# Keys and queries loaded as f32 by SyncE and cast by GpSimd, in place of GpSimd's casting loads

## The chip, the cores and the metric

The kernel runs on one core of one Trainium2 chip. A core has five engines with queues of their own: TensorE (PE in the profile; its weight loads are PEld) multiplies matrices, VectorE (DVE) and ScalarE (ACT) work on elements, GpSimd (POOL) does so too and can issue transfers, and SyncE (SP) issues transfers only. Every queue runs strictly in order, and engines wait for one another by semaphores. Transfers are carried by 16 DMA engines. The metric is the device time of one execution in microseconds (us): 232.63 us, the median of three runs (232.62 to 235.34).

## The reference

Two stages, in f32. Attention has a batch of 4, 8 heads, 768 positions and 64 values a head; heads 0, 2 and 6 see all earlier positions, the other five see the first 4 positions (the sinks) and a window of 64. A feed-forward block with a gate follows.

```python
scores = scale * np.matmul(q, k.transpose(0, 1, 3, 2))
causal = rel >= 0
stream_keep = causal & (is_sink | in_win)
scores = np.where(mask[None], scores, -1e9)
a = np.exp(scores - max); a = a / sum
attn = np.matmul(a, v)                       # (4, 8, 768, 64)
x = attn.transpose(0, 2, 1, 3).reshape(3072, 512)
h = x @ w_in                                 # 512 -> 2048
g = h * (1.0 / (1.0 + np.exp(-beta * h)))
return g @ w_out                             # 2048 -> 512, (3072, 512) f32
```

## The kernel before

**Units and chunks.** A chunk is one half (384 positions) of one batch; there are eight, 0 to 7. A chunk has four units, each a pair of heads p and p+4, so there are 32 units. For each unit the kernel needs keys and queries with the 64 head values on the partitions (transposed), in bf16. Scores are matmuls of transposed keys against transposed queries (L464 for units up to 11, L932 in groups for units 12 and up), exponents are taken on ScalarE (L472, L936), masks are multiplied in on VectorE (L437), the product with V (L495) is normed on VectorE (L498, L500) into x. x is transposed into xT, and the feed-forward block follows per chunk: first product (L560), tanh on ScalarE (L563), gate on VectorE (L566), second product (L604), output tile osb (L611 or L609), store (L614).

**How keys and queries arrive.** In chunks 0 to 2 they are loaded as f32 (`load_qk`, L138), cast to bf16 into `qkb` (`cast`, L296 on VectorE, L298 on GpSimd or ScalarE), and transposed by TensorE (L373). In chunks 3 to 7 they are loaded by GpSimd with a transfer that casts to bf16 on the way (`load_rows`, L330): 12 loads for a chunk, one for each of keys and queries, row block t of three, and half of the heads. They land in the rows tiles `ROWS[c % 2, name]`, two of which alternate. SyncE then issues transposing transfers from these rows into the key tile KT and the query tile QTD (`transposes_dma`, L341), six for a chunk, one for each of keys and queries and each t. A transposing transfer from SyncE also brings x to xT for units 8 and up, apart from unit 11 and the two units that end the program (`x_by_dma`, L511).

**What else stands on GpSimd.** V arrives as f32 by SyncE (`load_v`, L152, three loads of 256 KB for a chunk) and is cast into VX by GpSimd (L304; by VectorE for units 8 to 15). For the heads with a window, the sinks' keys are copied into KO (`sinks_of`, L356, L357, after the transposes), and the sinks' values into VO (L317, L318).

**What sets the order.** The order on every engine is written out by the program itself. A planned clock (`clock[0]`, in ns) goes forward by each TensorE step's planned cost. Work on other queues is put on a heap with a planned time (`later`, `event`) and is emitted once the clock has passed it. `rows_at` plans the loads of rows, `transposes_at` the transposes (never ahead of the rows' loads), `v_at` V's loads, `sinks_values` the sinks' copies and V's casts. From unit 12 on the scores are made in 13 groups, and what accompanies each is in a table of strings (SEQ). The planned times only set the order: on the chip each instruction runs when its queue reaches it and its semaphores allow it. TensorE's order is fixed in the same way. In the compiled program SyncE's transfers use eight completion semaphores in turn.

Chunk 3's scores are groups 0 to 2, chunk 4's 3 and 4, chunk 5's 5 and 6, chunk 6's 7 to 9, chunk 7's 10 to 12.

Of the kernel before, what the change touches and what calls it, by code (L numbers as in the profile page):

```python
# [17 lines left out]
def kernel(  # L18
# [13 lines left out]
    nc = tc.nc  # L32
# [253 lines left out]
    def cast(u, names=("k", "q"), on=None):  # L286
# [5 lines left out]
        for name in names:  # L292
            copy = on or nc.gpsimd.tensor_copy
            dst, src = s["qkb"][:, "qk".index(name)], staged[name, c, p // 2][:, p % 2]
            if copy == nc.vector.tensor_copy:
                copy(out=dst.rearrange("p t h d -> p h t d"), in_=src)  # L296
            else:
                copy(out=dst, in_=src.rearrange("p h t d -> p t h d"))  # L298
# [24 lines left out]

    def load_rows(c):

        b, h2 = chunks[c]

        def one(name, src, t, hh):
            r, w = h2 * HALF + t * 128, pos(b, hh) * D
            nc.gpsimd.dma_start(out=ROWS[c % 2, name][:, t].rearrange("p (a w) -> p a w", a=NPAIR)[:, :, w:w + D],  # L330
                                in_=src[b, hh * NPAIR:(hh + 1) * NPAIR, r:r + 128, :].rearrange("h p d -> p h d"))
        return [lambda n=n, src=src, t=t, hh=hh: one(n, src, t, hh) for n, src in (("k", k), ("q", q)) for t in range(HT) for hh in range(2)]
# [473 lines left out]
    rows3 = load_rows(3)  # L806
# [8 lines left out]
    for i in range(6):  # L815
        rows3[i]()
    for i in range(6, 9):
        later(1000 * (i - 3), rows3[i])
# [16 lines left out]
    def rows_at(at, some, gap=1000):  # L835
        for i, f in enumerate(some):
            event("rows", at + gap * i, f)

    def transposes_at(at, c, names=("k", "q"), gap=1300):
        for i, f in enumerate(transposes_dma(c, names)):  # L840
            f = event("transposes", at + gap * i, f, ("rows",))
# [3 lines left out]
    def v_at(at, c, tiles):  # L845
        for i in tiles:
            event("v", at + 2500 * i, lambda i=i: load_v(c, tiles=[i]))
# [6 lines left out]
    rows4 = load_rows(4)  # L854

    for t in range(8, 12):
# [4 lines left out]
        if t == 8:  # L861
            rows_at(1000, rows3[9:])
        if t == 9:
            transposes_at(0, 3, ("k",), 0)
        if t == 10:
            transposes_at(0, 3, ("q",), 0)
        if t == 10:
            rows_at(2000, rows4[0:4])
        if t == 11:
            rows_at(1000, rows4[4:8])  # L870
            for u in range(12, 16):
                sinks_values(u, 1000, 2000)
# [197 lines left out]
```

## Time and profile before

| | |
|---|---|
| median of three runs (lowest, highest) | 232.63 us (232.62, 235.34) |
| the profiled execution | 233.23 us |
| its span, from first to last instruction | 231.5 us |
| TensorE busy, granted clock | 218.4 us (94%), 1.0 |
| GpSimd busy, of it issues of the casting loads | 102.6 us, 45.0 us |
| read from and written to HBM | 27.27 MB, 6.29 MB |

One execution on the chip was recorded by the hardware profiler. The page gives each engine's busy time, then the span in 40 slices, then the chain of work that ended last, followed back from the last instruction, then the costliest groups of instructions. In a group's line stand the source line, the engine, the operation, what is written and read and in what shape (partitions x elements), how many, then the sum of their durations in us and the mean in ns, then the idle time of the engine just before them and what ended it. A line of the transfers gives KB each and the median us from issue to landing. In the timeline a line starts with the time of the start and the duration, both in us; SPq and POOLq are the queues of SyncE and GpSimd. In the tables by stretch, after the stretch and its length, come the busy times of TensorE, its weight loads, VectorE, ScalarE and GpSimd with the count of instructions, then the granted clock, the DMA share and GB/s. Matmuls are pipelined and their ends are modelled.

### The profile page before, as it was taken

The numbers are of one execution on the slowest core, as the hardware profiler recorded it, in microseconds if no ns is written. First come the engines' busy times: TensorE is split into PE (matmuls) and PEld (weight loads), VectorE is DVE, ScalarE is ACT, GpSimd is POOL, SyncE is SP. The second block draws the span as 40 slices with busy tenths as digits, with TensorE's granted clock in tenths as the row PEclk, the third lists the DMA queues.
The fourth block names the chain that finished last, engine by engine and source line by source line (L and its number), as shares of the span: only waits on it lengthen the run. The fifth ranks groups of instructions, "written<-read, shape, count | busy, mean of one in ns | idle before, by whom it ended". The sixth has DMA issues, their size and how long they took to land.

```text
span 231.5 us, 5309 instructions
## 1 busy us (share of the span) xinstructions
PE 218.4 (94%) x1939; PEld 131.5 (57%) x1960; DVE 143.7 (62%) x360; ACT 155.0 (67%) x303; POOL 102.6 (44%) x226
## 2 busy tenths in 40 slices
PE   7786799999999999999999999999999999999994
PEld 2675666555665566545654555454755555556553
DVE  6767578884968279835955594454781676338700
ACT  2897688866765798567875747775948797128621
POOL 6487760189619997219708793740042000000000
PEclk9999999999999999999999999999999999999999
DMA  6999999999999899994997999972732101211012
GB/s 193 258 302 192 165 168 219 222 225 227 193 148 137 115 139 144 125 218 109 152 191 126 146 184 140 143 136 71 172 64 62 50 0 45 77 50 50 0 45 91
DMA packets 96314, 31.78 MB, mean 137 GB/s; under 512 B 82704, under 2 KB 93344, under 8 KB 96288
## 3 DMA queue, kind: packets, MB, share of 16 engines
q0 software_dynamic: 35968, 8.13, 48.6%
q1 hardware_dynamic: 59456, 22.72, 47.9%
q10 hardware_dynamic: 864, 0.60, 0.8%
q8 instruction: 15, 0.25, 0.5%
q14 instruction: 11, 0.09, 0.2%
HBM read 27.27 MB, written 6.29 MB: 145 GB/s over the span
## 4 chain that ended last, share of the span: by engine, by line
PE 82%; DMA 4%; DVE 4%; issue 3%; ACT 3%; POOL 3%; POOLq 0%; ACTq 0%
PE mm L560 35%; PE tp L604 32%; PE po L495 5%; PE sp L932 5%; DMA w_in_sb<-in_moe_w_in_dram 4%; PE sp L464 2%; PE tp L587 2%; PE tp L373 1%; ACT es L936 1%; DVE es L437 1%; DVE x L500 1%; ACT es L472 1%; ACT th L563 1%; DVE KT L374 0%; PE tp L527 0%
## 5 line engine op out<-in xcount | busy, mean ns | idle before, releaser
L560 PE MATMUL mm<-xT,w_in_sb 128*128 128x384 bf16 x512 | 91.8, 326 | 1.8 <-DMA w_in_sb<-in_moe_w_in_dram 1.8
L563 ACT ACTIVATE th<-mm,beta_h 128x384 f32<-128x384 f32 x128 | 73.1, 598 | 22.1 <-PE mm L560 16.7
L604 PE MATMUL tp<-w_out_sb,gT 128*128 128x512 bf16 x347 | 86.5, 379 | 1.4 <-issue 0.3
L566 DVE SCALAR_TENSOR_TENSOR gT<-th,mm 128x384 bf16<-128x384 f32 x128 | 67.6, 551 | 30.5 <-ACT th L563 25.9
L560 PEld LDWEIGHTS <-w_in_sb 128*128 128x128 bf16 x512 | 48.0, 98 | 33.6 <-issue 2.2
L604 PEld LDWEIGHTS <-gT 128*128 128x128 bf16 x368 | 33.9, 98 | 33.6 <-issue 0.3
L936 ACT ACTIVATE es<-sp 128x512 bf16<-128x512 f32 (+1 forms) x84 | 39.9, 595 | 4.5 <-PE sp L932 4.5
L611 ACT ACTIVATE osb<-tp 128x512 f32<-128x512 f32 x21 | 12.7, 603 | 33.8 <-PE tp L604 30.5
L304 POOL CAST VX<-vs 128x384 bf16<-128x384 f32 x22 | 11.0, 508 | 36.7 <-DMA vs<-in_v_dram 32.2
L472 ACT ACTIVATE es<-sp 128x512 bf16<-128x512 f32 (+1 forms) x44 | 22.5, 561 | 4.3 <-PE sp L464 3.2
L495 PEld LDWEIGHTS <-es 128*128 128x128 bf16 x472 | 20.7, 97 | 7.8 <-issue 0.9
L330 POOL DMA_DIRECT2D s<-in_q_dram x30 | 22.5, 771 | 0.8 <-issue 0.6
L495 PE MATMUL po<-VX,es 128*128 128x65 bf16 x392 | 22.4, 193 | 0.3 <-DVE x L500 0.3
L330 POOL DMA_DIRECT2D s<-in_k_dram x30 | 22.5, 775 | 0.1
L437 DVE TENSOR_TENSOR es<-es,Mh 128x512 bf16<-128x512 bf16 (+3 forms) x58 | 19.5, 373 | 4.1 <-ACT es L936 3.7
L500 DVE TENSOR_TENSOR x<-po,rec 128x384 bf16<-128x384 f32 x32 | 17.8, 557 | 1.1
L464 PE MATMUL sp<-QTP,KT 128*128 128x128 bf16 (+2 forms) x113 | 16.6, 230 | 1.7 <-ACT es L472 0.9
L437 DVE TENSOR_TENSOR es<-es,Mc 128x384 bf16<-128x384 bf16 (+2 forms) x21 | 7.8, 374 | 11.4 <-ACT es L936 10.8
L498 DVE RECIPROCAL rec<-po 128x6 f32<-128x6 f32 x32 | 6.1, 192 | 13.2 <-PE po L495 13.1
L356 POOL COPY KO<-KT 128x128 bf16<-128x128 bf16 (+1 forms) x22 | 9.1, 412 | 9.6 <-DVE KT L374 5.5
L317 POOL COPY VO<-VX 128x128 bf16<-128x128 bf16 (+3 forms) x24 | 9.0, 374 | 8.6 <-DVE VX L304 7.6
L464 PEld LDWEIGHTS <-KT 128*128 128x128 bf16 x113 | 10.3, 98 | 3.6 <-issue 1.0
(75 smaller groups left out, 169.9 us busy)
## 6 DMA issues: line engine op xcount, KB each, us to landing
vs<-in_v_dram SPq DMA_DIRECT2D x24, 256.0 KB, 6.9
out_dram<-osb SPq DMA_DIRECT2D x23, 256.0 KB, 2.2
s<-in_k_dram SPq DMA_DIRECT2D x12, 192.0 KB, 4.3
w_in_sb<-in_moe_w_in_dram POOLq DMA_DIRECT2D x8, 256.0 KB, 8.3
w_out_sb<-in_moe_w_out_dram POOLq DMA_DIRECT2D x4, 512.0 KB, 11.1
s<-in_q_dram SPq DMA_DIRECT2D x10, 192.0 KB, 5.7
s<-in_k_dram POOLq DMA_DIRECT2D x30, 64.0 KB, 4.7
s<-in_q_dram POOLq DMA_DIRECT2D x30, 64.0 KB, 5.5
```

The source lines that it names most:

```text
L330: nc.gpsimd.dma_start(out=ROWS[c % 2, name][:, t].rearrange("p (a w) -> p a w", a=NPAIR)[:, :, w:w + D], in_=src[b, hh * NPAIR:(hh + 1) * ...
L437: nc.vector.tensor_mul(e, e, m)
L464: nc.tensor.matmul(sp[:, (i - lo) * 128:(j - lo) * 128], lhs, s["QT"][hh][:, q0 * 128:(q0 + j - i) * 128], start=True, stop=not added)
L472: nc.scalar.activation(out=es[:, 0:w], in_=sp[:, 0:w], func=ACTF.Exp, scale=scale)
L495: nc.tensor.matmul(po[:, qi, hh, :], e, val, start=(j == 0), stop=(j == len(lst) - 1))
L500: nc.vector.tensor_mul(x, po[:, :, :, 0:D], rec.to_broadcast([128, HT, 2, D]))
L560: nc.tensor.matmul(hp[:, 0:HALF], w_in_sb[:, mo, fi * 128:(fi + 1) * 128], xT[c][:, mo, :], start=(mo == 0), stop=(mo == MO - 1))
L563: nc.scalar.activation(out=th, in_=hp[:, 0:HALF], func=ACTF.Tanh, scale=beta_h[:, fi:fi + 1])
L566: nc.vector.scalar_tensor_tensor(out=gTs[c][:, fi, :], in0=th, scalar=1.0, in1=hp[:, 0:HALF], op0=ALU.add, op1=ALU.mult)
L604: nc.tensor.matmul(op, gTs[c][:, fi, ns * 128:(ns + 1) * 128], w_out_sb[:, fi, :], start=(fi == 0), stop=(fi == FO - 1))
L611: nc.scalar.activation(out=osb, in_=op, func=ACTF.Copy, scale=0.5)
L936: nc.scalar.activation(out=es[:, 0:w], in_=sp[:, 0:w], func=ACTF.Exp, scale=scale)
```

## The change

In chunks 3 to 7, `load_rows` no longer issues 12 casting loads on GpSimd. SyncE issues six f32 loads (keys and queries, three row blocks, all eight heads, 256 KB each), and GpSimd casts each to bf16 into the same rows tiles: one copy of 512 elements a partition, or, for the last batch (chunks 5 and 7), where the two halves of the heads change place, two copies of 256. Chunk 3's loads go into three small buffers (`fr`), which its keys and then its queries use; chunks 4 to 7 share one f32 tile each for keys and queries (`FROW`).

The planned times are written anew: chunk 3's keys are loaded ahead of its V, transposes wait for the casts instead of the loads, loads and casts of a chunk have times of their own (`chunk_at`), and the sinks' copies of a chunk come ahead of the next chunk's casts. V of chunk 4 is loaded at 75 instead of 88 us of planned time, with steps of 1.5 instead of 2.5 us. Last, `cast` uses one order of the axes on all engines: VectorE also writes its destination in one run and reads its source in the other order.

```diff
     def cast(u, names=("k", "q"), on=None):
...
-            if copy == nc.vector.tensor_copy:
-                copy(out=dst.rearrange("p t h d -> p h t d"), in_=src)
-            else:
-                copy(out=dst, in_=src.rearrange("p h t d -> p t h d"))
+            copy(out=s["qkb"][:, "qk".index(name)], in_=staged[name, c, p // 2][:, p % 2].rearrange("p h t d -> p t h d"))
...
     def load_rows(c):
-        def one(name, src, t, hh):
-            r, w = h2 * HALF + t * 128, pos(b, hh) * D
-            nc.gpsimd.dma_start(out=ROWS[c % 2, name][:, t].rearrange("p (a w) -> p a w", a=NPAIR)[:, :, w:w + D],
-                                in_=src[b, hh * NPAIR:(hh + 1) * NPAIR, r:r + 128, :].rearrange("h p d -> p h d"))
+        def load(name, src, t):
+            r = h2 * HALF + t * 128
+            if c == 3:
+                here[name, t] = stage.tile([128, H, D], F32, name="fr", bufs=3)
+            else:
...
+                here[name, t] = FROW[name][:, t]
+            nc.sync.dma_start(out=here[name, t], in_=src[b, :, r:r + 128, :].rearrange("h p d -> p h d"))
+
+        def cast_row(name, t):
+            out_ = ROWS[c % 2, name][:, t].rearrange("p (a w d) -> p w a d", a=NPAIR, w=2)
+            in_ = here[name, t].rearrange("p (w a) d -> p w a d", w=2)
+            if pos(b, 0) == 0:
+                nc.gpsimd.tensor_copy(out=out_, in_=in_)
+            else:
+                for hh in range(2):
+                    nc.gpsimd.tensor_copy(out=out_[:, pos(b, hh)], in_=in_[:, hh])
...
+    def rows_at(t1, t2, loads, casts, gap1=700, gap2=900):
+        for i, f in enumerate(loads):
+            event("rows", at(t1) + gap1 * i, f, ("casts",) if i == 0 else ())
+        for i, f in enumerate(casts):
+            event("casts", at(t2) + gap2 * i, f, ("rows",) if i + 1 == len(casts) else ())
...
-            event("v", at + 2500 * i, lambda i=i: load_v(c, tiles=[i]))
+            event("v", at(us) + 1500 * i, lambda i=i: load_v(c, tiles=[i]))
...
+    clock[0] = max(clock[0], 50000.0)
+    rows_at(51, 51, [], casts3[0:3], gap2=900)
+    transposes_at(54.5, 3, ("k",))
+    rows_at(52, 57.5, loads3[3:], casts3[3:], 900)
+    transposes_at(59.5, 3, ("q",))
+
+    def chunk_at(c, t1, t2, t3, names):
+        loads, casts = load_rows(c)
+        for n in names:
+            i = 0 if n == "k" else HT
+            rows_at(t1, t2, loads[i:i + HT], casts[i:i + HT])
+            transposes_at(t3, c, (n,))
+            t1, t2, t3 = t1 + 700 * HT / 1000, t2 + 900 * HT / 1000, t3 + 1250 * HT / 1000
...
             for u in range(12, 16):
-                sinks_values(u, 1000, 2000)
+                sinks_values(u, at(65.5), at(70))
+            chunk_at(4, 63.5, 68.5, 71, "qk")
...
-            v_at(at(88), 4, range(3))
-            rows_at(at(89), load_rows(5))
+            for i, u in enumerate((18, 16, 17, 19)):
+                sinks_values(u, at(86.5), at(94) + 1200 * i)
+            chunk_at(5, 82, 90, 102, "kq")
...
-            transposes_at(at(98), 5, gap=1200)
...
-            rows_at(at(113), load_rows(6), 750)
+            chunk_at(6, 111, 117, 123, "kq")
...
-            transposes_at(at(124), 6)
...
-            rows_at(at(134), load_rows(7), 750)
...
-            transposes_at(at(146), 7)
+            chunk_at(7, 138, 144, 150, "kq")
+            v_at(152, 7, range(3))
```

## The prediction

> **What bounds the kernel now.** I read the page's busy line first, then the chain, then TensorE stretch by stretch, then GpSimd's and SyncE's instructions around the loads that change.
>
> ```profile
> PE 218.4 (94%) x1939; PEld 131.5 (57%) x1960; DVE 143.7 (62%) x360; ACT 155.0 (67%) x303; POOL 102.6 (44%) x226
> PE 82%; DMA 4%; DVE 4%; issue 3%; ACT 3%; POOL 3%; POOLq 0%; ACTq 0%
> ```
>
> TensorE is busy 94% of the span, and the chain lies on it for 82%. Where are the other 13 us? The busy time by stretch (us from the start, then length, then each engine's busy time) says:
>
> ```profile
> 0.00:34.00 34.00, 26.43 (x344) 19.73 (x345) 23.99 (x72) 23.62 (x50) 24.02 (x78) 1.00 1.07 213
> 49.00:207.00 158.00, 155.80 (x1377) 90.22 (x1394) 97.21 (x244) 106.28 (x210) 75.27 (x144) 1.00 1.07 127
> 207.00:231.50 24.50, 21.14 (x131) 12.51 (x130) 9.51 (x18) 11.75 (x21) 0.00 (x0) 1.00 0.12 44
> ```
>
> 7.6 us of gaps lie before 34 us and 3.4 us after 207 us. The loads that change run from 46 to 146 us; between 49 and 207 us TensorE stands still for 158.00 - 155.80 = 2.2 us in all. That is the most that better loading can win there. There is no such limit on what late data can lose: TensorE's order is the same in both programs, so a late operand stops everything behind it.
>
> **GpSimd.** The groups of instructions by shape, and the transfers by issue:
>
> ```profile
> L330 POOL DMA_DIRECT2D s<-in_q_dram x30 | 22.5, 771 | 0.8 <-issue 0.6
> L330 POOL DMA_DIRECT2D s<-in_k_dram x30 | 22.5, 775 | 0.1
> L304 POOL CAST VX<-vs 128x384 bf16<-128x384 f32 x22 | 11.0, 508 | 36.7 <-DMA vs<-in_v_dram 32.2 <-issue 4.5
> L356 POOL COPY KO<-KT 128x384 bf16<-128x384 bf16 x10 | 5.6, 556 | 2.9 <-DMA KT<-s 2.9
> L356 POOL COPY KO<-KT 128x128 bf16<-128x128 bf16 x12 | 3.5, 291 | 6.6 <-DVE KT L374 5.5 <-DMA KT<-s 1.1
> vs<-in_v_dram SPq DMA_DIRECT2D x24, 256.0 KB, 6.9
> s<-in_k_dram POOLq DMA_DIRECT2D x30, 64.0 KB, 4.7
> ```
>
> Removed: 60 issues, 45.0 us. Added: 18 casts of 128x512 (chunks 3, 4, 6) and 24 of 128x256 (chunks 5 and 7, of the last batch, whose halves swap). No such shape is in the trace. The two L356 rows give (556-291)/256 = 1.04 ns per element; from the 508 ns cast of 384, I get 0.64 and 0.38 us: 18 x 0.64 + 24 x 0.38 = 20.5 us. Bounds: 0.29 us each (the shortest of these rows), 12 us, and twice 508 ns each, 43 us. Either way GpSimd loses work and is off the chain, so I cost it at nothing. What the casts bring is waiting: an issue waits for nothing, a cast waits for its load, and V's copies, the sinks' copies (L356, L317) and chunk 2's casts (L298) stand behind it in order. At chunk 3 the cast for unit 11 stands behind three casts whose loads I expect by 57 us (46.5, where the stage's transfers begin, plus 1.6 MB at the 222 GB/s of the page's slice, plus the 3.3 us of the shortest landing); TensorE transposes unit 11 at 66.0. V's copies for chunk 3 come out around 80 (78.2 before), their products start at 84.7. So the cover is several us; gone, it would cost the difference one for one.
>
> **SyncE and the transfers.** 30 loads of 256 KB join SyncE's queue. They have exactly the shape of V's loads (L152), whose issue takes 0.37 to 7.88 us, median 0.59, and whose landing 3.3 to 15.5. At the median that is 18 us more on a queue that also issues every transpose of keys and queries (L341), every transpose of attention output (xT, L511) and every store (L614), each in order behind whatever is ahead. HBM reads stay 7.7 MB (60 x 128 KB or 30 x 256 KB). For the change speaks that a packet of the software queue took 48.6% x 16 x 231.5 us / 35968 = 50 ns, of the hardware queue 47.9% / 59456, so 30 ns: the engines may do the same rows faster. Against it: latency. The compiled order gives SyncE's transfers eight completion semaphores in turn, so each issue also waits for the eighth before it, and a burst of six loads fills most of that.
>
> Now each handover, by the compiled order against the times of before. "Needed" is TensorE's first use.
>
> Chunk 3. Its K loads take the place of V's at 49.8 us, queries follow as casts free the three buffers (about 57 to 60), and its last query transpose starts near 69 (store at 64.9 as now, 0.5, three transposes of 1.2); now it is 68.0. With 3.7 us to land it is there by 74; needed 75.6. Cost 0, up to 2 if loads land like V's at this place (7.8 to 9.1 us).
>
> Chunk 2's third xT. Its input is ready at 74.8; six loads of chunk 4 now go out just ahead. Issued near 76, landing 4 to 6 instead of 3.0, it is there at 80 to 82; needed 82.1. I take 0.3, bounds 0 and 1.5.
>
> Chunk 4 gains: its last query transpose lands at 90.66 + 6.4 = 97.1 now. In the new order six transposes and three V loads, 9 us, follow the casts from about 78 on, so 5 us of landing later it is 92 to 93; needed 98.0. TensorE doesn't wait there, so nothing.
>
> Chunk 5. This is where the new planned time (102 instead of 98) shows. SyncE's queue and TensorE's chain:
>
> ```profile
> 102.31 3.92 SPq L341 DMA_TRANSPOSE KT<-s  x3
> 106.40 1.88 SPq L341 DMA_TRANSPOSE QTD<-s  x1
> 108.38 0.52 SPq L614 DMA_DIRECT2D out_dram<-osb  x1
> 109.06 2.58 SPq L341 DMA_TRANSPOSE QTD<-s  x2
> ...
> 120.86 1.77 SPq L511 DMA_TRANSPOSE xT<-x  x1
> ```
> ```profile
> 118.77 0.77 PE sp L932 x18
> ...
> 121.86 2.54 PE tp L604 x11
> 124.40 0.65 PE mm L560 x4
> ```
>
> Four transposes stand ahead of the store at 108.38 now; in the new order one does. The store waits for its output tile, so five transposes follow it: 109.0 plus five of 1.2 and one V load of 0.6, the last starts at 114.4. Landing 3.5 to 5.9 (this stage's rows) gives 117.9 to 120.3; needed 118.8. I take 0.6, bounds 0 and 2.
>
> Chunk 4's fourth xT. It is issued at 120.86 (behind the store at 120.23) and lands 3.7 us later, at 124.6; the product at 124.40 uses it in its fourth matmul, at 124.9. There is no slack. In the new order, three loads of chunk 6 and three of V go out between 114 and 119. In the stretch before, with V's loads and casting loads ahead, the same transposes took 4.6 to 7.1. So 0.6 to 3.1 late; bounds 0 and 3.1, and I take 0.9, near the 4.6 row, since some loads will have landed.
>
> Rule to weigh: the Trainium skill (DMA: Bandwidth & Descriptors, "Queues, rings and completion order") says that each DMA engine consumes one queue's descriptors in ring order and shares packets round robin between queues. By it, a transpose that now competes with loads on another queue would stand behind them, and the late end (3.1 us here, 1.5 at 82 us) would hold; the rows above mix both kinds of load and don't settle it.
>
> Chunks 6 and 7 start at 142 and 174 us. Their transposes start by 134 and 162, landing within 6: cost 0, cover 2 us and more.
>
> **VectorE's casts.** Ten casts (before: mean 512 ns, 340 to 809) read in another order. Bounds: 0.17 us saved each (down to 340), and 0.30 added (to the longest). Only two are waited for by TensorE (1.3 us, at the start); I take +0.2 for both, with bounds -0.3 and +0.6. The Trainium skill (VectorE: DVE Perf Modes, "What auto-detection actually checks") lets a copy use both ports only if the outermost sizes of source and destination are both even or equal; that speaks against this edit: source 3, destination 384 in the new order, against even ones before. By it all ten go to about the 555 ns of L374's copy; by the trace's mean they change by a twelfth.
>
> **Sum.** 0.3 + 0.6 + 0.9 + 0.2 = +2.0 us, against the profiled execution's own time: 231.5 span + 1.7 around = 233.2. It is 0.6 above the median of the runs, 232.63, so the forecast is 232.63 + 2.0 = **234.6**. Ends of the terms: -0.3 to 2 + 1.5 + 2 + 3.1 + 0.6 = +9.2.
>
> **Rivals.**
> 1. *Small loss, as above*, +0.5 to +4.6: 233.1 to 237.2. Chance 0.54.
> 2. *SyncE becomes the bound.* Its loads wait on casts, casts on loads, transposes on both; the late end then holds at most of the handovers. 232.63 + 5 to 9.2 = 237.6 to 242. For: issues of 3.8 and 7.9 us already occur in L152's rows when transfers back up. Against: 1.5 MB of casting loads go out between 46 and 58 us now, 0.8 MB in the new order. Chance 0.26. (The ring order of the Trainium skill's DMA page, above, would bring this case about.)
> 3. *Nothing on the path changes*: every landing falls within its cover, -0.3 to +0.5: about 232.7. The eight-semaphore wait and the store's place at 108.38 speak against it. Chance 0.15.
> 4. *Not slower but faster.* GpSimd's queue is no longer held in blocks of 4.5 us (six issues), so copies and xT go out sooner and the 2.2 us of gaps close: 230.4. It decides from the point where the fourth xT of chunk 4 lands within 3.7 us behind six loads. Against it: the list of waits puts only 0.7 us of TensorE's waits down to GpSimd's casts and 0.4 to V's load. Chance 0.05.
> That the edit does nothing is no case: 60 instructions go.
>
> **Chances.** 2% of 232.6 is 4.7 us, about what a measurement here tells from no change (the three runs lie 232.62 to 235.34). Slower by more: rival 2, 0.26. Faster by more would need 228, beyond the 2.2 us: 0.02. Within: 0.72. Range: 232.0 to 239.5, leaving out rival 4 and most of the top of rival 2.
>
> **What would show it.** Right: L330 gone; 42 casts near 0.64 and 0.38 us; TensorE idle ahead of the scores of chunk 5 (near 119 us) and ahead of the first product of chunk 4 (near 125), put down to DMA; no new gap before 75. Wrong: loads landing above 10 us at 50 to 60, then a gap before chunk 3's scores that delays all after it; or transposes landing in 3 us behind loads, then rival 3.

## The result, and the profile after

The changed kernel takes 241.88 us (median of four executions, 240.29 to 243.27), the kernel before in the same comparison 232.83 us: a ratio of 1.036, with a 95% interval of 1.026 to 1.046. It is slower, and outside the predicted range of 232.0 to 239.5. The profiled execution of the changed kernel is its fastest, 240.29 us with a span of 238.6, against 233.23 and 231.5 before: its trace shows 7.1 us of the difference. Of the three longer ones only the mean granted clock is on record, 0.983 (242.34 us), 0.992 (241.41) and 0.986 (243.27) beside 0.990. Some executions run long from end to end whatever the kernel, one of those below at a granted clock of 0.66 (327 us), and the ratios leave out every execution more than 1.5% above the fastest of its kernel.

The page of the changed kernel, busy time and granted clock, and the chain:

```profile
PE 222.0 (93%) x1960; PEld 132.2 (55%) x1960; DVE 147.5 (62%) x360; ACT 155.6 (65%) x303; POOL 78.5 (33%) x208
PEclk9999999999999989999999999999999999999998
PE 73%; DMA 10%; POOL 5%; DVE 4%; ACT 4%; issue 3%; SPq 1%; POOLq 0%
L343 POOL CAST s<-s 128x512 bf16<-128x512 f32 x12 | 7.6, 634 | 21.9 <-DMA s<-in_k_dram 13.6
L346 POOL CAST s<-s 128x256 bf16<-128x256 f32 x24 | 9.2, 410 | 14.8 <-DMA s<-in_k_dram 12.5
```

GpSimd is 24 us less busy, and its casts cost what the prediction took (634 and 410 ns, taken as 640 and 380). That bought nothing. The chain lies on TensorE for 73% instead of 82%, and on transfers for 10% instead of 4%, but these shares do not say where the time went: 11.3 us of the transfers (4.7%) are one load of V that landed at 25.8 us, where the marks below show no loss, and most of the 5% on GpSimd leads up to a wait at 140 us that was in truth one for VectorE (see the second loss). In the slice from 83.5 to 89.5 us, and in the last one, the granted clock is below nine tenths, which it was in no slice before the change.

Where was the time lost? VectorE's 32 reciprocals (L498 before, L517 after) come in the same order in both kernels, so the start of each is a mark. How far the changed kernel's marks lie behind the same marks of the kernel before, in us:

| mark, in the time of the kernel before | 74.0 | 86.5 | 95.2 | 110.3 | 118.0 | 133.5 | 164.7 | 172.4 | 205.3 |
|---|---|---|---|---|---|---|---|---|---|
| the changed kernel | 0.07 | 4.83 | 4.83 | 4.84 | 4.83 | 5.78 | 5.78 | 6.93 | 6.93 |

So there are three losses: 4.76 us between 74 and 86, 0.95 between 118 and 133, and 1.15 between 165 and 172. Everywhere else the two kernels run alike.

**First loss.** SyncE's queue in the kernel before and after (start and issue time in us), then TensorE after:

```profile
70.28 1.21 SPq L511 DMA_TRANSPOSE xT<-x  x1
...
72.21 3.76 SPq L511 DMA_TRANSPOSE xT<-x  x2
```
```profile
71.26 1.21 SPq L530 DMA_TRANSPOSE xT<-x  x1
...
73.83 2.07 SPq L337 DMA_DIRECT2D s<-in_q_dram  x3
75.99 0.82 SPq L633 DMA_DIRECT2D out_dram<-osb  x1
76.95 1.21 SPq L530 DMA_TRANSPOSE xT<-x  x1
78.20 2.90 SPq L337 DMA_DIRECT2D s<-in_k_dram  x3
81.22 1.48 SPq L530 DMA_TRANSPOSE xT<-x  x1
```
```profile
82.21 0.49 PE L579 MATMUL mm<-xT,w_in_sb 128*128 128x384 bf16 x2
86.07 0.48 PE L579 MATMUL mm<-xT,w_in_sb 128*128 128x384 bf16 x2 [3.37 <-DMA xT<-x]
```

The third transpose of xT was issued at 74.8 us and is now issued at 81.2, with six loads (2.07 + 2.90 us of issue) ahead of it on the queue. It lands 4.81 us later, at 86.03 (before: 2.96 us later, at 77.75), and TensorE waits 3.37 us for it. So of the 8.3 us by which it lands later, 6.4 are the place on the queue and 1.9 the transfer itself. The rest of the first loss, 1.4 us, is the clock. The table by stretch of the changed kernel (TensorE's busy time is the first number after the length, the granted clock stands behind the five busy times):

```profile
84.00:86.00 2.00, 0.00 (x0) 0.00 (x0) 0.55 (x1) 0.00 (x0) 0.62 (x2) 1.00 0.90 148
86.00:88.00 2.00, 1.93 (x29) 1.10 (x29) 0.79 (x2) 1.40 (x3) 0.34 (x1) 0.78 0.70 140
88.00:90.00 2.00, 2.00 (x19) 1.33 (x18) 1.04 (x4) 2.00 (x6) 0.00 (x0) 0.50 0.63 122
90.00:92.00 2.00, 2.00 (x26) 1.35 (x25) 0.68 (x3) 1.22 (x4) 0.00 (x0) 0.86 0.73 166
```

From 87.13 to 90.54 us TensorE gets half its clock, so the wait is paid for once more.

**Second and third loss.** VectorE's masks before, and then after (the `x7` line belongs to chunk 5's scores, the `x6` line to chunk 6's):

```profile
131.53 2.00 DVE L437 TENSOR_TENSOR es<-es,Mh 128x384 bf16<-128x384 bf16 x7
165.41 1.56 DVE L437 TENSOR_TENSOR es<-es,Mh 128x256 bf16<-128x256 bf16 x6
```
```profile
136.72 2.59 DVE L456 TENSOR_TENSOR es<-es,Mh 128x384 bf16<-128x384 bf16 x7
171.20 3.01 DVE L456 TENSOR_TENSOR es<-es,Mh 128x256 bf16<-128x256 bf16 x6
```

The same masks take 0.6 and 1.45 us longer. Both times TensorE then waits for x, which VectorE makes behind the masks: 0.90 us at 140.16 and 0.99 us at 175.98 (0.31 and nothing before). The profile puts the wait at 140.16 down to a GpSimd copy (L376) that ended 0.09 us earlier; but TensorE starts 0.15 us behind the end of x there, as it did in the kernel before (134.22 and 134.37), so x is what it waited for.

What else is new at these places is GpSimd. Beside the `x7` masks, from 136.4 to 140.1 us, it casts the last of chunk 5's values, copies its sinks' values and then chunk 6's sinks' keys; before, it copied sinks' keys to 132.9 us and then only issued loads. Chunk 7's values it casts and copies at 169 to 175 us, where it was idle from 155.3 to 170.5 us before.

The remaining 0.4 us of the second loss is a wait of 0.41 us at 130.12 for chunk 4's fourth xT. This part can't be put down to the change: the kernel before does not wait there in its own trace, but in three runs of it with edits elsewhere (below) it waits 0.24, 0.56 and 1.14 us for the same transpose.

### The profile page after: what moved, and what is told of

It is laid out like the page before. It is cut to its first block, busy times and chain, and to the rows that moved or that the text cites. A ratio compares the mean times of both kernels' runs of the same rounds, so it can differ in the third digit from the quotient of the medians.

```text
span 238.6 us, 5313 instructions
## 1 busy us (share of the span) xinstructions
PE 222.0 (93%) x1960; PEld 132.2 (55%) x1960; DVE 147.5 (62%) x360; ACT 155.6 (65%) x303; POOL 78.5 (33%) x208
## 3 DMA queue, kind: packets, MB, share of 16 engines
q0 software_dynamic: 4288, 4.20, 11.3%
HBM read 27.27 MB, written 6.29 MB: 141 GB/s over the span
## 4 chain that ended last, share of the span: by engine, by line
PE 73%; DMA 10%; POOL 5%; DVE 4%; ACT 4%; issue 3%; SPq 1%; POOLq 0%
PE mm L579 30%; PE tp L623 29%; PE po L514 5%; DMA vs<-in_v_dram 5%; PE sp L958 4%; PE sp L483 2%; DMA xT<-x 2%; PE tp L606 1%; DMA s<-in_k_dram 1%; DMA s<-in_q_dram 1%; ACT es L962 1%; POOL VX L300 1%; ACT th L582 1%; DVE gT L585 1%; PE tp L392 1%
## 5 line engine op out<-in xcount | busy, mean ns | idle before, releaser
L579 PE MATMUL mm<-xT,w_in_sb 128*128 128x384 bf16 x512 | 93.4, 329 | 5.0 <-DMA xT<-x 3.8
L623 PE MATMUL tp<-w_out_sb,gT 128*128 128x512 bf16 x368 | 89.4, 379 | 0.0
L456 DVE TENSOR_TENSOR es<-es,Mh 128x512 bf16<-128x512 bf16 (+3 forms) x58 | 22.0, 412 | 4.6 <-ACT es L962 3.4
L514 PE MATMUL po<-VX,es 128*128 128x65 bf16 x392 | 22.9, 195 | 1.0 <-POOL KO L376 0.9
L456 DVE TENSOR_TENSOR es<-es,Mc 128x384 bf16<-128x384 bf16 (+2 forms) x21 | 9.1, 435 | 11.5 <-ACT es L962 11.0
L300 POOL CAST VX<-vs 128x384 bf16<-128x384 f32 x22 | 11.6, 536 | 12.6 <-DMA vs<-in_v_dram 12.6
L517 DVE RECIPROCAL rec<-po 128x6 f32<-128x6 f32 x32 | 6.1, 192 | 15.2 <-PE po L514 15.2
L343 POOL CAST s<-s 128x512 bf16<-128x512 f32 x12 | 7.6, 634 | 21.9 <-DMA s<-in_k_dram 13.6
L346 POOL CAST s<-s 128x256 bf16<-128x256 f32 x24 | 9.2, 410 | 14.8 <-DMA s<-in_k_dram 12.5
L958 PE MATMUL sp<-QTD,KT 64*128 64x128 bf16 (+2 forms) x199 | 11.9, 233 | 0.3 <-ACT osb L630 0.3
```

The lines of the kernel that those rows point to most:

```text
L300: copy(out=VX[b % 2, p][:, h2 * HT:(h2 + 1) * HT, :, 0:D], in_=staged["v", c][:, :, p:H:NPAIR, :])
L456: nc.vector.tensor_mul(e, e, m)
L514: nc.tensor.matmul(po[:, qi, hh, :], e, val, start=(j == 0), stop=(j == len(lst) - 1))
L579: nc.tensor.matmul(hp[:, 0:HALF], w_in_sb[:, mo, fi * 128:(fi + 1) * 128], xT[c][:, mo, :], start=(mo == 0), stop=(mo == MO - 1))
L623: nc.tensor.matmul(op, gTs[c][:, fi, ns * 128:(ns + 1) * 128], w_out_sb[:, fi, :], start=(fi == 0), stop=(fi == FO - 1))
L958: nc.tensor.matmul(sp[:, a * 128:z * 128], lhs[half(h)], st_u[u]["QT"][half(h), q0 * 128:(q0 + z - a) * 128], start=True, stop=True)
```

## The experiments

Theory A is that the large loss is a matter of place in SyncE's queue. Its rivals are the bytes on the DMA engines, and GpSimd's casts. The second and third losses had a theory of their own: GpSimd's reads slow the masks. All results below are set beside executions of the kernel before on the same chip. The marks of all runs stand in one table behind the last of them.

### Chunk 4's keys behind the transposes

```diff
         for n in names:
             i = 0 if n == "k" else HT
+            if (c, n) == (4, "k"):
+                t1, t2, t3 = 71.5, 74.5, 76
             rows_at(t1, t2, loads[i:i + HT], casts[i:i + HT])
```

> The changed kernel, but chunk 4's three key loads stand behind chunk 2's third xT in SyncE's queue (planned at 71.5 us instead of 65.6, their casts at 74.5, their transposes at 76). Theory A (place in the queue): that transpose is issued at 78 to 79 us instead of 81.2 and lands by 83, the gap of 3.4 us at 82.7 shrinks below 0.5, and the granted clock, which fell to 0.50 to 0.86 behind the gap, stays at 1.0; the profiled time of 240.3 falls by 4 to 5 us to about 236. Rival B (transfers): chunk 4's query loads alone keep the 16 engines busy, the transpose still lands at 85 or later, and the time stays above 239.

Measured: 240.17 us (238.12 to 241.50), ratio 1.026 [1.020, 1.032]. The first loss is gone: the third transpose was issued at 79.08 us and landed 2.54 us later, not at 85 or later as by rival B, and at 95.2 us the lag is 0.31 us. But it comes back one handover later. The chain of this kernel, near 104 us:

```profile
102.13 0.57 SPq L337
...
103.37 0.81 SPq L337
...
104.29 3.98 DMA xT<-x
...
108.31 2.40 PE mm L579 x7
```

Now chunk 5's query loads (L337) stand ahead of chunk 3's last two transposes of xT. TensorE waits 3.86 us, and the granted clock is 0.50 from 106.7 to 113.6 us; the lag goes from 0.31 to 6.87 us. The theory holds for the place; the hope of 236 us did not, since it looked at one place.

### And chunk 7's values late again

```diff
         if gi == 7:
             chunk_at(7, 138, 144, 150, "kq")
-            v_at(152, 7, range(3))
         if gi == 9:
+            v_at(156, 7, range(3))
```

> As the run with chunk 4's keys behind, and chunk 7's V is loaded at the place where the kernel before loads it (behind the store at 162.9 us of its trace). Theory C (GpSimd's casts of V hold up VectorE's masks): the six masks of 128x256 that took 3.01 us at 171 take 1.6 again, the TensorE gap of 1.0 us before 176 goes, 1.0 to 1.3 us less than with the keys alone, so about 234.8 in the profile. Rival D (those masks are late for another reason, such as late exponents): the six masks stay near 3 us and nothing is won.

Measured: 238.47 us (236.23 to 239.65), ratio 1.019 [1.016, 1.022]. The six masks take 1.56 us again, as before the change, and the lag does not grow between 164.7 and 172.4 us (6.29 and 6.30). So the third loss hangs on the time at which chunk 7's values are loaded. The 234.8 us expected of this kernel did not come: the wait for xT near 104 us is still there, with 2.83 us at 108.13, and this trace has one more besides, 1.86 us at 76.40 for chunk 3's queries: TensorE was 1.1 us early there, while the last transpose of these queries was issued at 73.82 us, 1.3 us later than in the changed kernel. It makes 1.5 of the 2.2 us by which the lag grows up to 86.5 us.

### The kernel before, with chunk 7's values early

```diff
         if gi == 7:
             ...
+            v_at(at(152), 7, range(3))
         if gi == 9:
-            v_at(at(156), 7, range(3))
```

> The kernel before, with chunk 7's V loaded as early as in the changed kernel (planned at 152 us, ahead of two stores). Theory C: GpSimd casts V beside the masks of group 9, the six masks of 128x256 go from 1.56 to about 3.0 us and the time rises by 0.8 to 1.2 us to about 233.7. Rival D: nothing moves, 232.6 to 232.9.

Measured: 234.57 us (233.73 to 236.37), ratio 1.004 [1.001, 1.008]. The masks in this kernel, and GpSimd at the same time:

```profile
165.14 2.77 DVE L437 TENSOR_TENSOR es<-es,Mh 128x256 bf16<-128x256 bf16 x6
```
```profile
165.58 0.50 POOL L304 CAST VX<-vs 128x384 bf16<-128x384 f32 x1
166.14 0.65 POOL L317 COPY VO<-VX 128x384 bf16<-128x384 bf16 x1
166.86 0.78 POOL L318 COPY VO<-VX 4x384 bf16<-4x384 bf16 x1
```

With this one edit the masks grow from 1.56 to 2.77 us, and the lag by 0.9 us at that place. The third loss is reproduced alone.

### Reads or any work of GpSimd?

```diff
+        if u >= 28:
+            vx, vo = VX[b % 2, p], VO.get((b % 2, p))
+            nc.gpsimd.tensor_copy(out=vx[:, h2 * HT:(h2 + 1) * HT, :, 0:1], in_=staged["v", c][:, :, p:H:NPAIR, 0:1])
+            for _ in range(2):
+                nc.gpsimd.memset(vx[:, h2 * HT:(h2 + 1) * HT, :, 0:D], 0.5)
+                if streams[p]:
+                    nc.gpsimd.memset(vo[:, ka - 1:kz - 1, :, 0:D], 0.5)
+            return
         cast_v(u)
```
on the kernel before, with chunk 7's values early. This kernel leaves out chunk 7's values.

> The kernel before with chunk 7's values loaded at group 7 as in the earlier run of that edit, but chunk 7's casts of values and sinks' copies left out and replaced by GpSimd operations that read one column of the loaded values and then only write: two memsets of VX and two of VO for each pair (chunk 7's values are thus not computed). Theory (VectorE's masks, two operands read from SBUF, are slowed by GpSimd's reads from SBUF): the six masks 128x256 near 165 us, 1.56 us in the kernel before and 2.77 us with the casts beside them, take 1.6 to 1.8 us beside memsets. Rival (any work of GpSimd at the same time slows them, writes too): 2.3 us or more.

Measured: 233.59 us, ratio 0.999 [0.995, 1.003]. VectorE, and GpSimd beside it:

```profile
166.08 1.56 DVE L445 TENSOR_TENSOR es<-es,Mh 128x256 bf16<-128x256 bf16 x6
```
```profile
165.72 0.42 POOL L316 MEMSET VX<- 128x384 bf16 x1
166.07 0.26 POOL L318 MEMSET VO<- 128x192 bf16 x1
```

But for one read of a single column (0.21 us), GpSimd writes through nearly the whole of the masks, and they take 1.56 us: no longer than beside an idle GpSimd. So here it is reads that slow them. The Trainium skill (SBUF — State Buffer, "Who interferes with whom") says the same: a VectorE instruction with two inputs in SBUF contends with a GpSimd instruction that reads SBUF, and not with one that only writes it. The trace agrees, with 2.77 against 1.56 us.

### VectorE's casts alone

```diff
             copy = on or nc.gpsimd.tensor_copy
-            dst, src = s["qkb"][:, "qk".index(name)], staged[name, c, p // 2][:, p % 2]
-            if copy == nc.vector.tensor_copy:
-                copy(out=dst.rearrange("p t h d -> p h t d"), in_=src)
-            else:
-                copy(out=dst, in_=src.rearrange("p h t d -> p t h d"))
+            copy(out=s["qkb"][:, "qk".index(name)], in_=staged[name, c, p // 2][:, p % 2].rearrange("p h t d -> p t h d"))
```

> The kernel before, with only the axes of the casts changed as in the changed kernel (VectorE reads in another order and writes in one run). If VectorE loses a fast form, its ten casts go to about 0.5 us each without those of 0.35, and the time moves by -0.2 to +0.5 us; TensorE at 76 us was only 0.13 us later in the changed kernel, so I expect 232.7 to 232.9. If the axes matter more, a gap shows in the first 34 us.

Measured: 233.85 us, ratio 1.002 [0.999, 1.005]. A group's line of the kernel before, then of this one:

```profile
L296 DVE CAST qkb<-s 128x384 bf16<-128x384 f32 x10 | 5.0, 512 | 1.2 <-DMA s<-in_k_dram 1.1
```
```profile
L294 DVE CAST qkb<-s 128x384 bf16<-128x384 f32 x10 | 5.5, 556 | 1.6 <-DMA s<-in_k_dram 1.5
```

The mean moves by 44 ns, but it hides two kinds. Of the ten casts, five took 0.34 to 0.36 us before and the others up to 0.81; now nine take 0.54 to 0.55, and one 0.63. This is what the rule in the prediction gave (all ten at about 555). On the time it does not show. The only new wait of the trace between 46 and 207 us is one of 1.14 us at 125.69 for chunk 4's fourth xT; the last of the ten casts ends at 60 us, so I put it down to how much this wait varies in the kernel before.

### The loads on GpSimd's queue

```diff
-            nc.sync.dma_start(out=here[name, t], in_=src[b, :, r:r + 128, :].rearrange("h p d -> p h d"))
+            nc.gpsimd.dma_start(out=here[name, t], in_=src[b, :, r:r + 128, :].rearrange("h p d -> p h d"))
```
together with chunk 7's values late.

> The changed kernel, with two edits: all the f32 loads of keys and queries of chunks 3 to 7 are issued by GpSimd instead of SyncE (same buffers, same bytes, same casts), and chunk 7's values are loaded at group 9 as in the kernel before. Theory A (what is lost is lost in SyncE's order: 30 loads of 0.7 us and their places ahead of the transposes of xT): chunk 2's third xT is issued near 76 us and there is no gap on TensorE near 82 us over 0.5 us, none over 1 us near 104 us, the granted clock stays at 1.0 through both, the six masks near 166 us take 1.6 us. Only the 0.9 us at the masks of chunk 5's scores stays: 233 to 235 us. Rival B (the f32 loads hold up the transposes on the DMA engines, whoever issues them): the third xT still lands 4 to 5 us after its issue and after 84 us, and the gap stays: 237 to 240 us. Rival C (GpSimd becomes the bound, with 30 issues of 0.75 us in front of its casts): KT and QTD come late and the scores wait for them: 235 to 238 us.

Measured: 237.95 and 238.47 us in two executions, with a ratio of 1.020 [1.013, 1.027], and 242.32 and 249.32 us in two more; theory A's 233 to 235 us did not come. The trace is that of 242.32 us, so only its order is read. There is no wait near 82 us: with the same loads and casts, off SyncE's queue, the third transpose goes out at its old place (72.71 us and 3.98 us for two), and the first loss is gone. Two others take its place:

```profile
101.26 0.45 PE L958 MATMUL sp<-QTD,KT 64*128 64x128 bf16 x8 [1.90 <-DMA KT<-s]
133.13 0.48 PE L579 MATMUL mm<-xT,w_in_sb 128*128 128x384 bf16 x1 [3.00 <-DMA xT<-x]
```

The first is rival C: chunk 4's keys now wait in GpSimd's queue (loads issued 80.0 to 82.6 us, casts 86.8 to 89.4), and chunk 4's scores for them. The second is a transpose of xT that was issued at 124.91 us and took 8.18 us to land: rival B's effect, though at another place than it said, and in the one trace that there is. Which queue carries the loads decides where the kernel waits, not whether it does.

### One key load ahead instead of three

```diff
+            if (c, n) == (4, "k"):
+                t1, t2, t3 = 70, 71.2, 74.75
```

> The changed kernel with one instead of three of chunk 4's key loads ahead of chunk 2's third transpose of xT. Theory A (place in SyncE's queue): the wait for xT near 82 us, 3.37 us with three loads ahead, goes down by the two loads' issue time, to about 2 us; in the run with none ahead it was 1.0 us. What the granted clock does after a gap of about 2 us is open: after 1.0 us it stayed at 1.0, after 2.8 us and more it fell to 0.5.

Measured: 240.40 us (two executions, 240.24 and 240.55), ratio 1.028 [1.023, 1.033].

```profile
85.26 0.48 PE L579 MATMUL mm<-xT,w_in_sb 128*128 128x384 bf16 x2 [1.73 <-DMA xT<-x]
108.01 1.33 PE L579 MATMUL mm<-xT,w_in_sb 128*128 128x384 bf16 x7 [1.41 <-DMA xT<-x]
```

Three key loads ahead give a wait of 3.37 us and one gives 1.73. With none it is nothing in the run with the keys behind, 1.01 us in the one with V late as well, and 0, 0.76 and 0.78 us in the three kernels below that keep this order. So the wait follows the issue time ahead of the transpose, with a spread of 1.0 us between executions of one order; the landing has a part in it, 4.81 us behind three loads, 4.36 behind one, 2.53 to 4.24 behind none. After 1.73 us the clock stayed at 1.0, and the loss was the wait alone: the lag grew by 1.5 us instead of 4.8.

### Chunk 5's loads behind, too

```diff
-            chunk_at(5, 82, 90, 102, "kq")
+            chunk_at(5, 93, 100, 104, "kq")
```
on top of chunk 4's keys behind and chunk 7's values late.

> The kernel of the run with chunk 4's keys behind and chunk 7's values late, and also chunk 5's key loads behind three of chunk 3's transposes of xT and its query loads behind the fourth, all still on SyncE. Theory A (the second stall, at 104 to 108 us, is again the place of loads in SyncE's queue): the gap of 2.8 us near 105 us goes below 0.5 us and the granted clock stays at 1.0 there; some 3 us come back of 238.5: 235 to 236 us, if chunk 5's last QTD still lands by its scores (119 to 120 us). Rival (SyncE has no room left between 82 and 118 us, so that a load that goes behind one consumer is late for the next): the stall appears at chunk 5's scores near 119 to 122 us, as a wait for QTD or KT, with 1 to 3 us, and the time stays at 237 to 239 us.

Measured: 237.29 us (236.69 to 238.52), ratio 1.016 [1.011, 1.022]; the profiled execution has a span of 235.3 and the clock at 1.0 throughout. TensorE's waits:

```profile
82.73 0.48 PE L579 MATMUL mm<-xT,w_in_sb 128*128 128x384 bf16 x2 [0.76 <-DMA xT<-x]
105.36 0.97 PE L579 MATMUL mm<-xT,w_in_sb 128*128 128x384 bf16 x5 [0.93 <-DMA xT<-x]
127.12 0.49 PE L579 MATMUL mm<-xT,w_in_sb 128*128 128x384 bf16 x2 [1.23 <-DMA xT<-x]
```

The wait at 105 us shrinks from 2.83 to 0.93 us. The time stays above theory A's 235 to 236 us. Chunk 5's scores, where the rival looked, do not wait, but chunk 4's xT does, now at 127 us, for 1.23 + 0.37 us: each of these transposes has loads of chunk 6 ahead of it (without such loads on SyncE's queue the kernel before has waited up to 1.14 us here).

### Chunk 6's loads behind, in two ways

```diff
-            chunk_at(6, 111, 117, 123, "kq")
+            chunk_at(6, 119, 125, 127, "kq")
```
```diff
+            chunk_at(6, 115, 123, 125, "kq")
```
both on top of chunk 5's loads behind. By the first, all six loads stand behind chunk 4's four transposes of xT; by the second, the keys stand between the third and the fourth of them (the expectation had them ahead of the third).

> The kernel of the run with chunk 4's keys and chunk 5's keys and queries behind, and also chunk 6's loads (keys and queries) behind all four of chunk 4's transposes of xT, with chunk 6's casts behind chunk 5's casts of values on GpSimd. Theory A (each wait for xT is a place in SyncE's queue): the waits for xT of 1.23 and 0.37 us near 127 us go; 235.5 to 236 us, unless chunk 6's own scores then wait. Rival (no place is free: what stands behind chunk 4's transposes is late for chunk 6's scores, which the kernel before starts at 141.9 us): a wait for QTD or KT of 1 to 3 us near 143 us, and the time stays at 236.5 to 238.5 us. The masks of chunk 5's scores near 134 us, 2.57 us for seven before, go back to 2.0 us if it is the casts of values and queries beside them, and stay if the sinks' copies alone do it.

> As the run with chunk 6's loads behind all four of chunk 4's transposes of xT, but the key loads between the second and the third of them, and the queries behind the fourth. Theory A: the third and fourth transposes are late again by some 2 us of issue, so a wait for xT of 0.5 to 1.2 us near 127 us; chunk 6's scores start without a wait; 236 to 237 us. Rival (the issue time of SyncE is not what makes them late): no wait for xT, 235 us.

> The kernel with chunk 6's loads behind all four of chunk 4's transposes of xT once more, for a profile of it at the full clock (its ten timed runs had a median of 235.37 us). Theory A: waits for xT of 0.8 us near 82 us and 0.8 to 0.9 us near 106 us as in the two kernels it is made from, none near 127 us, seven masks near 133 us at 2.0 us: a span of 233.5 us, and 235.2 us. Rival (what is left of 1.7 us over the kernel before is spread over all stages): no single wait of over 0.5 us that the kernel before has not.

Measured, all behind: 235.37 us (ratio 1.007 [1.004, 1.010]) and, in the second comparison, 236.09 us (1.010 [1.004, 1.016]). The profiled execution of the first is that of 327 us, so the trace is that of the second (237.53 us, span 235.8). Keys between: 239.04 us, 1.022 [1.017, 1.027].

All behind, TensorE and VectorE:

```profile
106.56 0.97 PE L579 MATMUL mm<-xT,w_in_sb 128*128 128x384 bf16 x5 [1.89 <-DMA xT<-x]
146.11 0.98 PE L960 MATMUL sp<-QTD,KT 64*128 64x384 bf16 x16 [1.61 <-DMA QTD<-s]
134.02 2.04 DVE L456 TENSOR_TENSOR es<-es,Mh 128x384 bf16<-128x384 bf16 x7
169.57 1.56 DVE L456 TENSOR_TENSOR es<-es,Mh 128x256 bf16<-128x256 bf16 x6
```

Both sides had a part. The wait near 106 us, 0.93 us in the run above with the same order up to there, is 1.89 us here: again a spread of 1 us between executions. The waits near 127 us are gone, as theory A says, and chunk 6's scores now wait 1.61 us for their queries, as its rival says. With the keys between, the fourth transpose is issued at 126.95 us, behind three loads and a store, and TensorE waits for it:

```profile
130.47 0.32 PE L579 MATMUL mm<-xT,w_in_sb 128*128 128x384 bf16 x1 [3.23 <-DMA xT<-x]
```

I had given this 0.5 to 1.2 us. The seven masks are back at 1.94 us (keys between) and 2.04 us (all behind), and TensorE's wait behind them is 0.25 and 0.35 us instead of 0.90. Chunk 5's casts of values now run ahead of them; what stays beside them are the sinks' copies in the one and the casts of queries, with pauses, in the other. In the run with the loads on GpSimd's queue, where GpSimd stands still beside them, they take 1.63 us. So the part of the second loss that stands behind the masks goes when GpSimd reads less beside them; which of its reads counts most was not separated.

### Chunk 4's queries behind

```diff
+            if (c, n) == (4, "k"):
+                t1, t2, t3 = 72.5, 76, 78
...
-            chunk_at(4, 63.5, 68.5, 71, "qk")
+            chunk_at(4, 70, 74.5, 76.5, "qk")
```
on top of chunk 6's loads behind all four.

> As the kernel with chunk 6's loads behind, and of chunk 4's three query loads only one ahead of chunk 2's third transpose of xT, two behind it, with its key loads behind these. Theory A: the third transpose is issued 1.4 us earlier, the wait of 0.8 us near 82 us goes, 234.5 us, the same as the kernel before within its noise. Rival (no place is free): chunk 4's KT or QTD now come late for its scores near 100 us, a wait of 1 to 3 us there: 236 to 238 us.

Measured: 238.85 us (237.09, 237.29, 240.41, 240.49), ratio 1.025 [1.017, 1.033]. The trace is that of the execution of 237.09 us. In it no wait for xT near 82 us is left, and chunk 4's scores do not wait either: at 95.2 us the lag is -0.08 us. The two other waits stay:

```profile
106.12 0.97 PE L579 MATMUL mm<-xT,w_in_sb 128*128 128x384 bf16 x5 [2.08 <-DMA xT<-x]
145.70 0.98 PE L960 MATMUL sp<-QTD,KT 64*128 64x384 bf16 x16 [1.65 <-DMA QTD<-s]
```

Neither side of the expectation came: the place was free, and yet the kernel is not faster. Two of its executions took 3 us more than the other two, at a mean granted clock of 0.991 and 0.986 instead of 0.997 and 1.000; behind which waits the clock fell in them stays open, since they have no trace.

### The marks of the runs

How far each lies behind the kernel before at the same marks, in us (profiled executions; the start of the program varies by up to 1 us either way, so differences along a row count):

| mark | 74.0 | 86.5 | 95.2 | 110.3 | 118.0 | 133.5 | 164.7 | 172.4 | 205.3 |
|---|---|---|---|---|---|---|---|---|---|
| the changed kernel | 0.07 | 4.83 | 4.83 | 4.84 | 4.83 | 5.78 | 5.78 | 6.93 | 6.93 |
| one key load ahead | 0.91 | 2.42 | 2.41 | 4.15 | 4.25 | 5.95 | 5.94 | 6.89 | 6.88 |
| chunk 4's keys behind | -0.15 | -0.10 | 0.31 | 6.87 | 6.86 | 7.02 | 7.03 | 8.17 | 8.16 |
| and V late | -1.13 | 1.09 | 1.50 | 5.45 | 5.44 | 6.29 | 6.29 | 6.30 | 6.29 |
| and chunk 5 behind | -0.65 | -0.11 | 0.31 | 1.02 | 1.11 | 3.62 | 3.61 | 3.62 | 3.62 |
| and chunk 6 behind | -0.27 | -0.21 | 0.20 | 2.27 | 2.34 | 2.53 | 4.16 | 4.16 | 4.15 |
| and chunk 4's queries behind | -0.69 | -0.49 | -0.08 | 1.96 | 2.02 | 2.09 | 3.75 | 3.76 | 3.75 |
| chunk 5 behind, chunk 6's keys between | 0.81 | 1.38 | 1.79 | 2.37 | 2.46 | 5.48 | 5.48 | 5.48 | 5.48 |
| loads on GpSimd's queue, V late | 0.72 | 0.77 | 1.40 | 4.76 | 5.51 | 9.10 | 9.10 | 9.11 | 9.10 |
| kernel before, V early | -0.44 | -0.43 | -0.42 | -0.42 | -0.41 | -0.27 | -0.28 | 0.64 | 0.63 |
| kernel before, memsets | 0.16 | 0.17 | 0.17 | 0.17 | 0.17 | 0.67 | 0.67 | 0.67 | 0.67 |
| kernel before, VectorE's casts | -0.33 | -0.32 | -0.33 | -0.33 | -0.32 | 0.40 | 0.40 | 0.40 | 0.40 |

Read down a column, a loss disappears as its loads go behind; read along a row, it turns up at the next handover. The last two rows show how far single executions differ: between 118.0 and 133.5 us the kernel before loses 0.5 and 0.7 us in them, with edits that touch nothing there. No version here beats the kernel before. The nearest, with chunk 6 behind, keeps all of the change but the places of its loads and casts, and stands 1.7 and 2.4 us above the kernel before in its two comparisons, where the changed kernel stands 9.0 above it.

## Why the prediction was wrong, point by point

The forecast was rival 1, a small loss. What came is rival 2, SyncE becomes the bound, whose 237.6 to 242 us hold the measured 241.88; it had a chance of 0.26. But it did not come as it was told there, with the late end at most of the handovers: two thirds of the loss lie at one.

- **Chunk 2's third xT (0.3 us taken, bounds 0 and 1.5): 4.8 us. This is the step that failed.** Its landing was right (4 to 6 us; it took 4.81). Its issue was not: "near 76", and it was at 81.2. The prediction itself had the median issue of such a load, 0.59 us, and said that 18 us join SyncE's queue; but at this step, which says that six loads go out just ahead, it did not add them. They took 4.97 us, and a store and a transpose stand between them. By its own row, 74.8 + 6 x 0.59 = 78.3, plus 1.2 for the second transpose and 0.5 for a store, is 80.0; plus 4 to 6 us of landing is 84 to 86, against its own need at 82.1. One sum of numbers at hand would have given 1.9 to 3.9 us. That the place on the queue is the cause is shown by the runs with none, one and three of the key loads ahead (0 to 1.0, 1.73 and 3.37 us of waiting), and by the one with the loads on the other queue (none).
- **What no step named: the clock after a wait.** 1.4 of the 4.8 us came after the wait, with 3.41 us at a granted clock of 0.50.
- **Chunk 3 (0) and chunk 4 (nothing):** right for the changed kernel: no wait before 82 us is new, and none for chunk 4's scores. For chunk 3 the cover is thin: with V late its queries came 1.86 us late in one execution.
- **Chunk 5 (0.6, bounds 0 and 2): 0.** The lag is the same at 95.2 and at 118.0 us. Since everything ran 4.8 us late, the margin was wider than reckoned; it was not tested without that.
- **Chunk 4's fourth xT (0.9, bounds 0 and 3.1): 0.41.** Right in place and within its bounds, but by luck as far as one trace tells: "there is no slack" holds for the kernel before too, whose runs wait 0 to 1.14 us there, so 0.41 us does not show the change. That loads ahead of it can cost much more is shown by the keys between, with 3.23 us.
- **GpSimd's casts "off the chain, so I cost it at nothing": the second such error.** Their length was right, their waits were not the trouble, but where they run was: at 140 us TensorE waits 0.6 us longer behind VectorE's masks, and the wait goes back to 0.25 and 0.35 us when GpSimd reads less beside them.
- **Chunks 6 and 7 (0):** the cover of their transposes was right. The step looked at transposes alone; with them V moved to group 7, and its casts came to lie beside the masks of chunk 6's scores: 1.15 us in the changed kernel, 0.9 alone in the kernel before.
- **VectorE's casts (+0.2):** the changed kernel's mark lies 0.07 us behind at 74 us, and the edit alone has a ratio of 0.999 to 1.005. The trace's mean, "a twelfth", was right as a mean; the rule of the Trainium skill (VectorE: DVE Perf Modes, "What auto-detection actually checks") was right for the casts that had been fast, 0.35 to 0.55 us.
- **Rivals 3 and 4** fell with the first loss. The words "there is no such limit on what late data can lose" were the ones to follow.

The sum as measured: 0.07 + 4.76 + 0.95 + 1.15 = 6.93 us, the lag at the last mark, where 2.0 was forecast; the spans differ by 7.1. It is the sum of one pair of traces: of its terms 4.76 and 1.15 are shown by runs that take them away, while 0.4 of the 0.95 lies within what the kernel before does by itself.

## What to carry to other kernels

Price the issue time of every load on the queue that it joins, at each consumer whose transfer stands behind it: six loads of 0.6 to 1.3 us cost nothing until one late transpose is the operand that the busiest engine takes next. When a load goes behind one consumer, look at once at the next; on a queue with no room left the wait only moves. And an engine that is off the path can still cost time by the moment at which it reads memory: keep GpSimd's copies and casts away from VectorE's two-operand instructions that something waits for.

## What was unexpected of the hardware

**The clock fell after a wait of 1.9 us and not after one of 3.2.** Waits of 3.37 us (the changed kernel), 3.86 (chunk 4's keys behind), 2.83 (V late), and 1.90 and 3.00 (the loads on GpSimd's queue) came with a granted clock of 0.50, from inside the wait on or from at most 1.1 us behind it; one of 3.23 us (chunk 6's keys between) did not, and neither did those of 2.08, 1.89 and 1.86 us. The traces show what decides. Each stretch at 0.50 that ends ahead of the program's end lasts 3.41 us, or twice that after 3.86 us of waiting. Within one trace the starts of such stretches lie whole multiples of 3.413 us apart: 87.13 and 237.32 us in the changed kernel (44 of them), 101.61 and 132.33 us in the kernel with the loads on GpSimd's queue (nine). So a trace can be cut into stretches of 3.41 us, and TensorE's work in each be set beside the clock in the next. First the wait of 1.90 us, which ended at 101.26 us, then that of 3.23 us, which ended at 130.47 us and lay across two stretches:

```profile
98.20:101.61 3.41, 1.51 (x24) 0.79 (x22) 0.79 (x3) 0.98 (x2) 2.56 (x6) 1.00 1.08 92
101.61:105.03 3.42, 3.42 (x15) 1.23 (x10) 1.57 (x5) 2.07 (x4) 0.90 (x2) 0.50 1.08 257
```
```profile
125.21:128.62 3.41, 2.04 (x11) 0.88 (x9) 2.11 (x7) 0.91 (x2) 1.88 (x5) 1.00 1.17 239
128.62:132.04 3.42, 1.56 (x9) 0.83 (x9) 0.56 (x1) 0.58 (x1) 1.43 (x4) 1.00 1.08 278
132.04:135.45 3.41, 3.41 (x35) 1.78 (x34) 1.11 (x2) 1.62 (x4) 1.84 (x3) 1.00 1.15 192
```

Between 46 and 207 us of all these traces TensorE was busy for 1.06 to 1.51 us of the stretch ahead of each fall, and for 1.55 us or more of every stretch at the full clock that no fall followed. At half clock, 1.84 us of work did not bring it back (the second stretch after 3.86 us). The mark is not as sharp everywhere: at 23.92 us, in the run with one key load ahead, the clock fell behind 1.71 us of work.

Where the clock fell, it cost 1.1 us (2.83 us of waiting, 3.95 lost), 1.4 us (3.37, 4.76) and 2.7 us (3.86, 6.56) on top: four to five tenths of the time at 0.50 that was left behind the wait (2.7, 3.4 and 5.3 us). The Trainium skill (TensorE: Matmul & The Clock Gate, "What's actually happening") tells of an activity window of about 3.4 us that runs freely, and of a throttled clock behind a window that is idle. On the window the traces agree, with 3.413 us; that a window with up to 1.51 us of work in it is idle enough is what the measurement adds, and there it decides.

**A slow mask shows only in a stretch.** VectorE's masks by GpSimd's reads took 2.77 and 3.01 us instead of 1.56, nearly twice as long; in the page's group, over all 58, the mean moves from 373 to 412 ns.
